# Clustered attention and an MLP on one core: the weighted values of a pair of heads in one run

## The chip, the core and the metric

The kernel runs on one core of a Trainium2 chip. Its time is the device time of one execution in microseconds (us). Three runs of the kernel before took 932.9, 934.0 and 934.55 us, median 934.0. One more execution was profiled.

The engines have these names in the profile: PE is TensorE (PEld its weight loads), DVE VectorE, ACT ScalarE, POOL GpSimd, SP SyncE, which here only starts transfers.

## The reference

Four batches, eight heads, 768 positions, 64 elements a head. Queries and keys are each assigned to the nearest of 16 centroids of their head; a query sees only the keys of its own cluster. The result, 512 wide, goes through a mix over the positions of rank 32 and an MLP of 512 to 2048 to 512.

```python
mask = q_assign[:, :, :, None] == k_assign[:, :, None, :]
scores = np.where(mask, scale * (q @ k.T), -1e9)
attn = exp(scores - max(scores)); attn = attn / (sum(attn) + 1e-9)
x = attn @ v                                  # all heads side by side: (4, 768, 512)
u = x + (xt @ U @ V).T                        # xt is x transposed, the mix over positions
out = u + np.maximum(u @ w_ch1, 0.0) @ w_ch2
```

## The kernel before

Two heads of one batch make a pair; 16 pairs (0 to 15) are worked through one after the other, four to a batch. For one pair the steps are these, each a small function of the kernel:

- `load` fetches the queries and keys into the tile R, `load_v` the values into vt. `split_hi` and `split_lo` split R into a rounded part and its remainder (in the tile arena, L797 and L802), and the `place_` functions move rows of it by transfers on SyncE's queue.
- `sims` (L760) multiplies by the centroids, and `clusters` (eight steps on VectorE, L770 to L789) makes one-hot rows of the nearest one. These rows are added to keys and queries, so that a pair of one cluster scores far above all others.
- `rowmax` (L875) computes scores of 128 queries by 384 keys for the maximum of each query, which VectorE takes from the bank (L877), 24 times a pair. `rowmax_T` and `rowmax_place` turn the maxima (L887) into a row of the operands of `scores`.
- `scores` (L899, L901) computes 128 keys by 768 queries in four matmuls, and ScalarE takes the exp into a buffer pr (L904), 12 times a pair.
- `values` (L922) multiplies an exp by the values: two matmuls side by side in the array, 64 columns each, into the bank o_ps. Six of them, one for each 128 keys, add up to half a pair. `weights` (L914, GpSimd mostly) adds up the exps for the denominators in the tile T.
- `sums`, `sums_T` (L934, L942) and `normalise` (L955, L956) finish the pair; `turn_x` and `store_x` write it out. For each batch, `mix_u`, `mix_sum` and `mix_v` follow (L980 to L1005).

Row maxima and scores read operands of the type fp32r and use the whole array. Values, similarities and sums are f32, and 64 or 32 columns wide; several run side by side. Transposes are f32 with the whole array. The profile lists an f32 matmul that is not a transpose as two records.

What is left of the banks of the accumulator by the scores (two buffers of two banks) are four banks, in turn for row maxima, values, similarities, sums and transposes (`work`).

Behind the attention stands the MLP of batch 0 (`gemm1`, `after_gemm1`, `gemm2`), then the other three batches with weights that are combined in between (`seven1`, `seven2` and their helpers).

The order of everything is written out by hand. Each step is an event with a time in steps of the plan; 12 steps are one pair, M0 (193) is where the MLP begins. The tables `times`, `mixes` and `stages` give a base time by step and kind of pair, and `shifts` moves single events. The events are sorted by time and issued in that order, and each engine keeps it: an engine waits at the head of its queue, and all behind it wait as well. In this plan the values of a pair stand in two groups, one behind each six scores, and the row maxima of the next pair are spread between the scores by the list `spots`.

Of the kernel before, what the change touches and what calls it, by code (L numbers as in the profile page):

```python
# [59 lines left out]
    "load0":           (-34.78, -31.87, -43.62,   None,   None, -25.08),  # L60
    "load1":           (-26.35, -29.08, -32.88,   None,   None, -24.23),
    "sims":            ( -25.34, -28.59, -28.55,   None,   None, -21.62),
    "place_clusters":  (-17.02, -15.36, -15.03, None, -8.7, -12.43),
    "split_hi0":       (-29.17, -30.78, -24.16,   None,   None, -23.84),
    "split_lo0":       (-23.33, -24.18, -23.58,   None,   None, -18.16),
    "split_hi1":       (-23.81, -24.01, -24.25,   None,   None, -18.05),
# [5 lines left out]
    "load_v":          ( -19.68,  -4.35,  -7.21,   None, -23.16,  -9.16),  # L72
    "rowmax":          (-14.93, -14.94, -14.87, -5.2, -8.0, -11.36),
    "rowmax_T":        (-3.27, -3.31, -3.81, 0.8, 0.23, -2.00),
    "rowmax_place":    (-2.26, -2.12, -2.82, 1.0, 1.84, -1.34),
    "scores":          (     0,  -0.95,  -0.37,  -1.30,   0.99,   0.07),
    "weights":         (  1.45,  -0.11,   0.32,   0.76,   3.19,   1.68),
    "values":          (  1.45,   1.51,   0.02,   1.05,   3.14,   2.27),
    "sums":            ( 14.31,  14.69,  13.43,  15.42,  15.27,  14.98),
    "sums_T":          ( 15.73,  15.65,   14.20,  16.05,  17.52,  16.44),  # L80
    "normalise0":      ( 21.14,  17.04,  14.88,  21.88,  20.90,  21.40),
    "normalise1":      ( 22.35,  16.83,  15.64,   27.11,  21.03,  19.88),
    "clusters":        (-23.85, -25.21,  -23.10,   None,   None, -20.35),
# [13 lines left out]
    "g0":   ( 34.93,  36.55,  42.58,  52.94),  # L97
# [10 lines left out]
    "scores 14 1 3": -0.9,  # L108
    "turn_x 7 1": 0.26,
    "recover 7 1 1 0": 0.52,  # L110
    "mix_T 1 3 1": 0.27,
    "clusters 2 4": -0.66,
    "turn_u 0 3": 1.01,
    "values 5 1 0": -1.54,
    "rowmax 6 3 1": -4.17,
    "rowmax 10 2 0": -1.29,
    "normalise 6 1": -3.47,
    "clusters 3 7": 2.95,
    "scores 11 1 4": 0.73,
# [12 lines left out]
    "scores 2 0 0": 0.47,
    "split_lo 4 0": 0.77,
    "seven2 3 3 6": -0.13,
    "rowmax 2 4 0": -0.71,
    "rowmax_place 15 0 12": -0.73,
    "fetch_w2 6 0 3 4 5": -0.15,
    "load_mix 0 3": 1.15,
    "load_weights 1 6 3": 0.37,
    "scores 9 0 0": 0.29,  # L140
    "normalise 14 0": -1.4,
    "recover 7 1 1 1": 0.22,
    "load_weights 1 0 2": 1.44,
    "scores 14 1 4": -0.69,
    "rowmax 3 8 0": 0.26,
    "turn_x 7 0": 0.24,
    "fetch_w2 7 0 3 4 5": 0.19,
    "rowmax 3 5 1": 2.44,
    "rowmax 3 3 1": -0.83,
    "normalise 12 0": -0.59,  # L150
    "scores 15 1 2": -0.7,
    "values 5 0 0": -0.29,
    "values 5 0 1": -0.29,
    "values 5 0 2": -0.29,
    "values 5 0 3": -0.29,
    "values 5 0 4": -0.29,
    "values 5 1 1": -0.29,
    "values 5 1 2": -0.29,
    "values 5 1 3": -0.29,
    "values 5 1 4": -0.29,  # L160
    "rowmax 2 1 0": -0.55,
    "rowmax 3 3 0": -0.22,
    "rowmax 5 7 0": 2.33,
    "clusters 11 0": -1.58,
    "scores 12 1 1": 0.42,
    "scores 3 0 4": -0.07,
    "rowmax 3 1 1": 0.87,
    "sums 14": 0.54,
    "scores 10 1 1": -0.12,
    "clusters 15 1": -0.21,  # L170
    "rowmax 13 1 0": -1.15,
    "split_lo 7 0": 0.66,
    "normalise 4 0": -1.22,
    "load_weights 1 2 3": -0.16,
    "rowmax 6 8 0": 1.78,
# [1475 lines left out]
```

## Time and profile before

| | |
|---|---|
| median of three runs | 934.0 us (932.9 to 934.55) |
| profiled execution | 933.45 us |
| its span, first to last instruction | 931.6 us |
| TensorE busy | 910.3 us, 98% |
| VectorE busy | 733.7 us, 79% |
| GpSimd busy | 607.7 us, 65% |
| ScalarE busy | 449.2 us, 48% |
| mean granted clock of TensorE | 0.988 |
| moved by transfers | 206.26 MB |

Busy time is the time in which an engine has an instruction under way. A matmul's record overlaps the next one, so the time that one takes up in the queue is read from the start of one row to the start of the next. All durations come from the one profiled execution, so a sum is made against its 933.45 us.

### The profile page before, as it was taken

The numbers are of one execution on the slowest core, as the hardware profiler recorded it, in microseconds if no ns is written. First come the engines' busy times: TensorE is split into PE (matmuls) and PEld (weight loads), VectorE is DVE, ScalarE is ACT, GpSimd is POOL, SyncE is SP. The second block draws the span as 40 slices with busy tenths as digits, with TensorE's granted clock in tenths as the row PEclk, the third lists the DMA queues.
The fourth block names the chain that finished last, engine by engine and source line by source line (L and its number), as shares of the span: only waits on it lengthen the run. The fifth ranks groups of instructions, "written<-read, shape, count | busy, mean of one in ns | idle before, by whom it ended". The sixth has DMA issues, their size and how long they took to land.

```text
span 931.6 us, 15094 instructions
## 1 busy us (share of the span) xinstructions
PE 910.3 (98%) x5157; PEld 756.2 (81%) x5157; DVE 733.7 (79%) x1391; ACT 449.2 (48%) x803; POOL 607.7 (65%) x459
## 2 busy tenths in 40 slices
PE   5899999999999999999999999999999999999997
PEld 1666666776666666767899999999999999999997
DVE  6899888888888887698866355767879778887777
ACT  6454554555555545566656533542435424263330
POOL 3467687889789987773457936832487524865333
PEclk7899999999999999999999999999999999999999
DMA  7485655676768674368989997798776998679643
GB/s 210 109 203 129 185 132 123 206 186 172 198 156 190 175 185 112 92 204 275 281 283 318 291 324 266 263 338 269 236 281 211 355 252 311 231 254 327 234 174 114
DMA packets 122925, 206.26 MB, mean 221 GB/s; under 512 B 46528, under 2 KB 90240, under 8 KB 118368
## 3 DMA queue, kind: packets, MB, share of 16 engines
q1 hardware_dynamic: 122464, 205.20, 71.8%
q8 instruction: 41, 0.67, 0.3%
q14 instruction: 36, 0.29, 0.1%
q10 hardware_dynamic: 384, 0.10, 0.0%
HBM read 131.96 MB, written 42.83 MB: 188 GB/s over the span
## 4 chain that ended last, share of the span: by engine, by line
PE 93%; DVE 4%; DMA 2%; ACT 1%; issue 1%; SPq 0%; DVEq 0%; ACTq 0%
PE o_ps L922 14%; PE ps_max L875 8%; PE st L899 7%; PE st L901 6%; PE ps_p L1289 3%; PE ps_p L1290 3%; PE ps_p L1291 3%; PE ps_q L1365 3%; PE ps_q L1366 3%; PE ps_q L1367 3%; PE ps_q L1289 3%; PE ps_q L1291 3%; PE ps_q L1290 3%; PE ps_p L1365 3%; PE ps_p L1367 3%; PE ps_p L1366 3%
## 5 line engine op out<-in xcount | busy, mean ns | idle before, releaser
L914 POOL TENSOR_TENSOR T<-T,pr 128x768 f32<-128x768 f32 x120 | 223.9, 1866 | 31.5 <-ACT pr L904 11.3
L877 DVE TENSOR_REDUCE m<-ps_max 128x1 f32<-128x384 f32 x384 | 195.0, 546 | 45.3 <-PE ps_max L875 43.4
L904 ACT ACTIVATE pr<-st 128x768 f32<-128x768 f32 x192 | 154.6, 812 | 90.7 <-PE st L901 76.9
L922 PE MATMUL o_ps<-pr,vt 128*64 128x384 f32 x768 | 133.6, 492 | 0.1
L875 PE MATMUL ps_max<-arena 128*128 128x384 f32 x384 | 121.1, 380 | 8.5 <-DVE arena L840 6.2
L875 PEld LDWEIGHTS ps_max<-arena 128*128 128x128 f32 x384 | 70.5, 196 | 51.5 <-DVE m L877 18.1
L899 PE MATMUL st<-arena 128*128 128x384 f32 x384 | 103.3, 350 | 0.4 <-ACT pr L904 0.3
L922 PEld LDWEIGHTS o_ps<-pr,vt 128*64 128x64 f32 x768 | 51.2, 136 | 64.6 <-issue 60.3
L901 PE MATMUL st<-arena 97*128 97x384 f32 x384 | 98.9, 339 | 0.6 <-DMA arena<-mT 0.6
L914 POOL TENSOR_TENSOR T<-pr 128x768 f32<-128x768 f32 x30 | 56.1, 1869 | 47.3 <-ACT pr L904 47.3
L899 PEld LDWEIGHTS st<-arena 128*128 128x128 f32 x384 | 66.9, 189 | 7.8 <-issue 2.4
L901 PEld LDWEIGHTS st<-arena 97*128 97x128 f32 x384 | 70.6, 189 | 0.9 <-DMA arena<-mT 0.9
L1289 PE MATMUL ps_p<-arena,w 128*128 128x384 f32 x186 | 62.2, 334 | 0.0
L1291 PE MATMUL ps_p<-arena,w 128*128 128x384 f32 x186 | 62.2, 334 | 0.0
L1290 PE MATMUL ps_p<-arena,w 128*128 128x384 f32 x186 | 62.2, 334 | 0.0
L926 ACT COPY os<-o_ps 128x384 f32<-128x384 f32 x32 | 15.4, 481 | 78.1 <-PE o_ps L922 78.0
L1289 PE MATMUL ps_q<-arena,w 128*128 128x384 f32 x150 | 50.2, 335 | 0.0
L1291 PE MATMUL ps_q<-arena,w 128*128 128x384 f32 x150 | 50.2, 334 | 0.0
L1290 PE MATMUL ps_q<-arena,w 128*128 128x384 f32 x150 | 50.1, 334 | 0.0
L802 POOL TENSOR_TENSOR arena<-R,arena 128x768 fp32r<-128x768 f32 x16 | 35.0, 2186 | 15.7 <-ACT arena L797 15.6
L1351 POOL TENSOR_TENSOR h<-ring,h 128x384 fp32r<-128x384 f32 x17 | 17.7, 1041 | 38.6 <-ACT h L1341 19.6
L1290 PEld LDWEIGHTS ps_p<-arena,w 128*128 128x128 f32 x186 | 34.9, 188 | 0.1
(580 smaller groups left out, 2363.0 us busy)
## 6 DMA issues: line engine op xcount, KB each, us to landing
w<-wc SPq DMA_DIRECT2D x24, 1024.0 KB
w<-wc SPq DMA_DIRECT2D x25, 768.0 KB
arena<-wc SPq DMA_DIRECT2D x19, 768.0 KB
rw<-in_w SPq DMA_DIRECT2D x27, 512.0 KB
R<-in_qk SPq DMA_DIRECT2D x32, 384.0 KB
arena<-arena SPq DMA_DIRECT2D x31, 384.0 KB
arena<-arena SPq DMA_DIRECT2D x62, 192.0 KB
wc<-f SPq DMA_DIRECT2D x46, 256.0 KB
```

Of the source, the lines that this page charges most:

```text
L875: nc.tensor.matmul(ps[:, 0:HS], x1[:, 0, g // 2, g % 2, t * P:(t + 1) * P], x1[:, 1, h, g % 2, :], start=True, stop=True)
L877: nc.vector.reduce_max(live["m2", i][:, h, u:u + 1], ps[:, 0:HS], axis=AX.X)
L899: nc.tensor.matmul(st[:, j, 0:HS], x1[:, 1, hk, j, ks], x1[:, 0, h, j, :], start=True, stop=False)
L901: nc.tensor.matmul(st[:, j, 0:HS], x2[0:97, 1, hk, j, ks], x2[0:97, 0, h, j, :], start=False, stop=True)
L904: nc.scalar.activation(pr, st[:, :, 0:HS], AF.Exp, scale=SCALE)
L914: eng.tensor_add(T, live["p", i, h, 0] if c == 1 else T, live["p", i, h, c])
L922: nc.tensor.matmul(o_ps[64 * j:64 * j + 64, 0:HS], vv[:, c, j, :], pr[:, j, :], start=(c == 0), stop=(c == NT - 1))
L1289: nc.tensor.matmul(ps, w[:, 0, k], u[:, 0, k], start=(k == 0), stop=False)
L1290: nc.tensor.matmul(ps, w[:, 0, k], u[:, 1, k], start=False, stop=False)
L1291: nc.tensor.matmul(ps, w[:, 1, k], u[:, 0, k], start=False, stop=(k == 1))
L1365: nc.tensor.matmul(ps, w[:, 0], h[:, 0], start=(j == 0), stop=False)
L1366: nc.tensor.matmul(ps, w[:, 0], h[:, 1], start=False, stop=False)
```

## The change

The exps of a pair get twelve buffers in place of eleven, and the values two in place of three. From pair 3 to pair 13 the values of a pair stand together at step 11.5 of the pair, behind its twelve scores. The row maxima of pairs 4 to 14 come at an even pace of 0.41 steps from the start of the pair before, the eight cluster steps of a pair directly one behind the other. The base times change for the first pairs and for others, and the table `shifts` grows from about 420 entries to some 1570, up to the middle of batch 0's MLP. No instruction is added or removed, and none changes its engine.

```diff
-    "sims":            ( -25.34, -28.59, -28.55,   None,   None, -21.62),
+    "sims": (-24.51, -24.51, -24.51, None, None, -21.62),
...
-    "normalise0":      ( 21.14,  17.04,  14.88,  21.88,  20.90,  21.40),
+    "normalise0": (23.2, 17.04, 14.88, 21.88, 20.90, 23.2),
...
-    "scores 14 1 3": -0.9,
+    "scores 14 1 3": -2.38745455,
...
-        live["v", i] = sb.tile([P, NT, 2, D], F32, name="vt", bufs=3)
+        live["v", i] = sb.tile([P, NT, 2, D], F32, name="vt", bufs=2)
...
-        pr = sb.tile([P, 2, HS], F32, name="pr", bufs=11)
+        pr = sb.tile([P, 2, HS], F32, name="pr", bufs=12)
...
+    RUN, ROW0, PACE, LO, HI = 11.5, 0.33, 0.41, 3, 13
...
-                at(when("clusters", i) + 0.7 * k, clusters, i, k)
+                at(when("clusters", i) + (0.7 if i < 3 else 0.02) * k, clusters, i, k)
...
+                elif LO < i <= HI + 1:
+                    at(NS * (i - 1) + ROW0 + PACE * (2 * u + h), rowmax, i, u, h)
...
-            at(when("values", i) + GV * (k // GV) + GV - 1 + 0.03 * (k % GV), values, i, h, c)
+            if LO <= i <= HI:
+                at(NS * i + RUN + 0.005 * k, values, i, h, c)
+            else:
+                at(when("values", i) + GV * (k // GV) + GV - 1 + 0.03 * (k % GV), values, i, h, c)
```

TensorE's order around the values of pair 7, first of the kernel before. L899 and L901 are scores, L875 a row maximum, L760 the similarity of a later pair, L922 the values.

```order
L875 MATMUL ps_max<-arena 128x384 x2
L760 MATMUL ps_sim<-R,cT 32x384 x4
L875 MATMUL ps_max<-arena 128x384
L899 MATMUL st<-arena 128x384 x2
L901 MATMUL st<-arena 128x384 x2
L875 MATMUL ps_max<-arena 128x384 x2
L899 MATMUL st<-arena 128x384 x2
L901 MATMUL st<-arena 128x384 x2
L875 MATMUL ps_max<-arena 128x384
L922 MATMUL o_ps<-pr,vt 64x384 x12
L875 MATMUL ps_max<-arena 128x384 x2
```

The same place in the changed kernel; L2052 and L2054 are scores there, L2028 a row maximum, L2040 the transpose of the maxima, L1913 the similarity, L2075 the values.

```order
L2052 MATMUL st<-arena 128x384 x2
L2054 MATMUL st<-arena 128x384 x2
L2028 MATMUL ps_max<-arena 128x384 x2
L2040 MATMUL ps_mT<-ident,m 12x128
L1913 MATMUL ps_sim<-R,cT 32x384 x4
L2075 MATMUL o_ps<-pr,vt 64x384 x24
L2028 MATMUL ps_max<-arena 128x384 x2
L2052 MATMUL st<-arena 128x384 x2
```

Twelve matmuls of half a pair, with the similarity apart, have become 24 of a whole pair with the similarity and the transpose right before them.

VectorE's order for the clusters of pair 10, first before: L770 to L786 are cluster steps, L802 a split, L877 a row maximum.

```order
L770 STREAM_TRANSPOSE ps_sim<-ps_sim 128x384
L802 TENSOR_TENSOR arena<-R,arena 128x768
L776 TENSOR_REDUCE most<-ps_sim 128x24
L877 TENSOR_REDUCE m_2600<-ps_max 128x1 x2
L780 TENSOR_TENSOR ps_sim<-ps_sim,most 128x384
L877 TENSOR_REDUCE m_2600<-ps_max 128x1
L782 TENSOR_TENSOR ps_sim<-ps_sim,rank 128x384
L877 TENSOR_REDUCE m_2600<-ps_max 128x1 x2
L776 TENSOR_REDUCE most<-ps_sim 128x24
```

And in the changed kernel, beside the run of pair 7; L1745 to L1748 unpack a piece of weights, L1955 is the split, L2030 a row maximum.

```order
L1923 STREAM_TRANSPOSE ps_sim<-ps_sim 128x384
L1929 TENSOR_REDUCE most<-ps_sim 128x24
L1933 TENSOR_TENSOR ps_sim<-ps_sim,most 128x384
L1935 TENSOR_TENSOR ps_sim<-ps_sim,rank 128x384
L1929 TENSOR_REDUCE most<-ps_sim 128x24
L1939 TENSOR_TENSOR oh<-ps_sim,most 128x12x16 x2
L2120 STREAM_TRANSPOSE xs_2624<-xt 128x384
L1745 TENSOR_SCALAR ps_t<-rw_g 128x512
L1746 SCALAR_TENSOR_TENSOR ps_t<-rw_g,ps_t 128x512
L1748 SCALAR_TENSOR_TENSOR rw_t<-rw,ps_t 128x512
L1955 TENSOR_TENSOR arena<-R,arena 128x768
L2030 TENSOR_REDUCE m_2532<-ps_max 128x1 x2
```

The reductions that stood between the cluster steps have moved away; weights and split stand behind the steps instead.

At the start of the program TensorE's order was this (L694 turns the centroids, L887 the maxima of pair 0).

```order
L694 MATMUL ps_c<-ident,rw_g 128x128
L760 MATMUL ps_sim<-R,cT 32x384 x4
L875 MATMUL ps_max<-arena 128x384 x4
L694 MATMUL ps_c<-ident,rw_g 128x128
L875 MATMUL ps_max<-arena 128x384 x4
L694 MATMUL ps_c<-ident,rw_g 128x128
L875 MATMUL ps_max<-arena 128x384 x2
L760 MATMUL ps_sim<-R,cT 32x384 x4
L694 MATMUL ps_c<-ident,rw_g 128x128
L875 MATMUL ps_max<-arena 128x384 x2
```

In the changed kernel L1847 turns the centroids, L1913 is the similarity, and L2052 the first score.

```order
L1847 MATMUL ps_c<-ident,rw_g 128x128
L1913 MATMUL ps_sim<-R,cT 32x384 x4
L1847 MATMUL ps_c<-ident,rw_g 128x128
L1913 MATMUL ps_sim<-R,cT 32x384 x4
L1847 MATMUL ps_c<-ident,rw_g 128x128
L2028 MATMUL ps_max<-arena 128x384 x12
L1847 MATMUL ps_c<-ident,rw_g 128x128
L2028 MATMUL ps_max<-arena 128x384
L2040 MATMUL ps_mT<-ident,m 6x128
L2028 MATMUL ps_max<-arena 128x384 x2
L1847 MATMUL ps_c<-ident,rw_g 128x128
L2028 MATMUL ps_max<-arena 128x384 x3
```

The second similarity has moved ahead of the row maxima of pair 0, and twelve of these stand together. Up to the first scores nine more row maxima follow in the kernel before, and none beyond these rows in the changed one.

## Rows read from the trace of the kernel before

**Rows 1.** The page's busy times: us (share of the span) and instructions of each engine.
```profile
PE 910.3 (98%) x5157; PEld 756.2 (81%) x5157; DVE 733.7 (79%) x1391; ACT 449.2 (48%) x803; POOL 607.7 (65%) x459
```
**Rows 2.** Stages: us, busy PE, PEld, DVE, ACT, POOL (instructions), clock, DMA share, GB/s.
```profile
200.00:250.00 50.00, 50.00 (x310) 34.48 (x311) 44.68 (x90) 28.39 (x42) 44.70 (x25) 1.00 0.70 191
500.00:550.00 50.00, 50.00 (x254) 45.52 (x253) 22.01 (x38) 22.78 (x43) 39.35 (x31) 1.00 1.00 293
```
**Rows 3.** The values' line: count, ns min/median/max, first and last start.
```profile
L922 PE MATMUL o_ps<-pr,vt x768: 486/486/537, 38.8 to 430.2; 128*64 128x384 f32 x192
```
**Rows 4.** TensorE's timeline around half a pair's values: start us, us, engine, line, tiles, records.
```profile
331.27 0.55 PE L955 MATMUL ps_oT<-ident,os 128*128 128x128 f32 x3
331.58 0.59 PE L899 MATMUL st<-arena 128*128 128x384 f32 x2
332.01 0.52 PE L901 MATMUL st<-arena 97*128 97x384 f32 x2
332.37 0.52 PE L875 MATMUL ps_max<-arena 128*128 128x384 f32 x2
332.82 4.09 PE L922 MATMUL o_ps<-pr,vt 128*64 128x384 f32 x24
336.84 0.62 PE L875 MATMUL ps_max<-arena 128*128 128x384 f32 x2
337.30 0.51 PE L899 MATMUL st<-arena 128*128 128x384 f32 x2
```
**Rows 5.** The same timeline at a short run of values.
```profile
68.22 0.87 PE L922 MATMUL o_ps<-pr,vt 128*64 128x384 f32 x4
69.02 0.44 PE L875 MATMUL ps_max<-arena 128*128 128x384 f32 x1
```
**Rows 6.** The same timeline at transposes between fp32r matmuls.
```profile
202.86 0.49 PE L955 MATMUL ps_oT<-ident,os 128*128 128x128 f32 x3
203.10 0.42 PE L875 MATMUL ps_max<-arena 128*128 128x384 f32 x1
203.36 0.27 PE L887 MATMUL ps_mT<-ident,m 128*12 128x128 f32 x1
```
**Rows 7.** The same timeline at transposes in front of values.
```profile
127.77 0.49 PE L955 MATMUL ps_oT<-ident,os 128*128 128x128 f32 x3
128.23 0.87 PE L922 MATMUL o_ps<-pr,vt 128*64 128x384 f32 x4
```
**Rows 8.** Two windows of the first 70 us, columns as in rows 2.
```profile
14.00:24.00 10.00, 8.43 (x26) 4.07 (x26) 7.09 (x15) 5.93 (x17) 5.77 (x16) 0.50 0.94 259
60.00:70.00 10.00, 9.79 (x57) 7.50 (x56) 9.90 (x25) 6.24 (x10) 8.36 (x5) 1.00 0.72 199
```
**Rows 9.** VectorE's waits from 14 to 65 us: us in total, times, longest.
```profile
DVE m L877 <- PE ps_max L875: 3.8, 8, 1.6
DVE ps_sim L770 <- PE ps_sim L760: 1.2, 1, 1.2
```
**Rows 10.** The page's groups, GpSimd's adds: busy us, mean ns, idle before.
```profile
L914 POOL TENSOR_TENSOR T<-T,pr 128x768 f32<-128x768 f32 x120 | 223.9, 1866 | 31.5 <-ACT pr L904 11.3
```
**Rows 11.** VectorE's groups by line, 100 to 400 us: busy us, mean ns, idle before.
```profile
L877 DVE TENSOR_REDUCE m<-ps_max 128x1 f32<-128x384 f32 x286 | 146.2, 546 | 38.0 <-PE ps_max L875 36.3
L802 DVE TENSOR_TENSOR arena<-R,arena 128x768 fp32r<-128x768 f32 x11 | 16.7, 1518 | 0.0
...
L789 DVE STREAM_TRANSPOSE ohT<-oh 128x768 f32<-128x768 f32 x11 | 10.6, 965 | 0.0
...
L593 DVE SCALAR_TENSOR_TENSOR ps_t<-rw_g,ps_t 128x512 int32<-128x512 int32 x10 | 7.0, 696 | 0.3
```
**Rows 12.** VectorE on the similarity's bank: window, us, busy (instructions), clock, DMA share, GB/s.
```profile
200.00:250.00 50.00, 6.78 (x14) 1.00 0.70 191
```
**Rows 13.** TensorE's longest waits from 65 to 440 us: us in total, times, longest.
```profile
PE st L901 <- DMA arena<-mT: 0.6, 1, 0.6
```
**Rows 14.** TensorE's timeline at the first scores.
```profile
29.88 0.84 PE L899 MATMUL st<-arena 128*128 128x384 f32 x2
```

More of the change, by code (lines that the diff above doesn't have):

```diff
@@ L145 @@
[L145 to L146 removed]
+    "load_weights 1 0 2": 0.6475,
+    "scores 14 1 4": -1.111875,
+    "rowmax 3 8 0": -2.24,
     "fetch_w2 7 0 3 4 5": 0.19,
[L148 to L175, printed above, removed]
-    "clusters 3 6": -0.52,
-    "sums_T 14": 0.99,
@@ new lines @@
+    "rowmax 3 11 0": -0.39361111,
+    "rowmax 3 4 1": 3.48,
+    "weights 2 1 1": 0.238,
+    "scores 2 1 4": -2.8975,
+    "rowmax 3 7 1": -4.95005556,
+    "scores 2 0 5": 2.11175926,
+    "rowmax 3 7 0": 2.67263889,
+    "values 2 0 0": -0.07550926,
+    "split_hi 5 0": 1.75666667,
+    "load_v 4": 19.38333333,
+    "sums_T 1": 2.1184375,
+    "rowmax 3 9 1": 1.13078704,
+    "rowmax 4 1 1": 4.85333333,
+    "rowmax 4 3 0": 1.46466667,
+    "load 6 0": -9.8356,
+    "load_mix 2 3": 2.67080128,
@@ new lines @@
+    "rowmax 10 8 1": -6.225,
+    "rowmax 10 0 0": 0.78318182,
+    "scores 9 0 2": -0.88818182,
+    "rowmax 10 9 1": -4.01166667,
+    "rowmax 10 5 1": -3.72,
+    "rowmax 10 7 1": 2.17909091,
+    "rowmax 10 10 0": -0.00922078,
+    "store_x 7 1": 9.04083333,
+    "rowmax 10 2 1": 6.34824675,
+    "rowmax 10 4 0": 4.565,
+    "rowmax 10 0 1": 0.35,
+    "load 13 0": -4.20974026,
+    "scores 9 1 0": 4.44666667,
+    "weights 8 1 5": 0.65636364,
+    "sums 8": -0.78333333,
+    "rowmax 10 7 0": -5.47905303,
@@ new lines @@
+    "values 9 0 3": 0.30045455,
+    "values 9 0 4": 0.30863636,
+    "values 9 0 5": 0.31681818,
+    "normalise 8 1": 0.65113636,
+    "rowmax 11 4 1": 5.36636364,
+    "rowmax 11 2 1": -2.3305,
+    "place_keys_lo 12": -5.03852273,
+    "place_queries 12": -4.30113636,
+    "scores 10 0 1": -1.07909091,
+    "weights 9 1 2": 2.85375,
+    "weights 9 1 3": 1.9415,
+    "rowmax 11 11 0": -9.32213333,
+    "load 14 0": -2.16076923,
+    "rowmax 11 2 0": -2.05897727,
+    "rowmax 11 9 0": -7.494,
@@ new lines @@
+    "values 1 1 5": -0.02,
+    "scores 2 1 1": -4.4212,
+    "scores 2 1 0": 1.12171296,
+    "weights 2 0 3": 2.50986111,
+    "weights 2 0 4": 7.419375,
+    "values 2 0 1": -0.0946875,
+    "values 2 0 2": -0.123125,
+    "normalise 1 1": -0.495,
+    "load 6 1": 6.07111111,
+    "values 2 1 0": -0.1903125,
+    "values 2 1 1": -0.1809375,
+    "values 2 1 2": -0.19125,
+    "values 2 1 3": -0.07730769,
+    "weights 2 1 2": -0.686,
+    "values 2 1 4": -0.1000641,
+    "values 2 1 5": -0.12644231,
@@ new lines @@
+    "scores 5 0 2": -1.03571429,
+    "rowmax 6 9 1": -1.22533333,
+    "values 5 1 0": -0.63,
+    "scores 6 0 0": 2.37125,
+    "rowmax 8 5 0": -11.96305455,
+    "rowmax_T 7 0 12": -5.59991169,
+    "scores 7 0 3": -3.0834375,
+    "weights 7 0 1": -2.205,
+    "sums 6": -2.53,
+    "scores 7 1 2": 3.34625,
+    "clusters 10 5": 0.00872727,
+    "rowmax 9 3 1": -2.79090909,
+    "scores 8 0 2": -0.658125,
+    "weights 8 0 2": -2.069375,
+    "scores 8 0 3": -1.17142857,
+    "weights 8 0 4": -2.77857143,
```

1851 lines of the change are left out of this document (1477 added, 374 removed).

## The prediction

> **What bounds the kernel now.** I read the page's busy shares first: TensorE is busy 910.3 of 931.6 us [rows 1]. A share of the whole span says little about a stage, so the table of stages came next. From the middle of the attention part to its end TensorE works through whole windows (50.00 of 50 us at 200 to 250), at a granted clock of 1.00, while VectorE has 44.68 and GpSimd 44.70 us in the same window [rows 2]. In the MLP stage at 500 to 550 it is again 50.00 of 50, with the DMA engines at a share of 1.00 [rows 2]. So the end of the program is set by the length of TensorE's own queue nearly everywhere, and an order can only win what is lost between its matmuls. Two places lose something: the seams between kinds of matmul (below), and the first 70 us, where TensorE is not the limit. Sixteen pairs of heads pass in 38.8 to 430.2 us [rows 3], 24.5 us each; VectorE and GpSimd fill some 0.89 of that, so neither is far behind.
>
> **What a seam costs.** In the timeline of TensorE two fp32r matmuls of 384 columns take 0.36 us from start to start (332.01 to 332.37). The same two in front of the values take 0.45 (332.37 to 332.82), and directly behind the values 0.46 (336.84 to 337.30) [rows 4]: 0.09 us on the way in, 0.10 behind the way out. A run of values has a fixed part as well. 24 records last 4.02 us [rows 4], 4 records 0.80 [rows 5], so a record costs (4.02 - 0.80) / 20 = 0.161 us and every run 0.80 - 4 x 0.161 = 0.16 us on top. One stretch of values between fp32r matmuls thus loses 0.35 us. Similarities and sums, 32 columns wide, I take to behave alike.
>
> The Trainium skill, TensorEngine Tiling (Array Packing), Key Properties, says that a change of the tiling mode drains the engine. The trace agrees: the losses sit at both ends of a run, and by that rule and by the rows alike a run twice as long pays once.
>
> Transposes between fp32r matmuls cost 0.24 for three and 0.08 on the next matmul (0.26, against half of 0.36), 0.32 in all [rows 6]. Directly behind tiled matmuls three cost 0.31 and 0.07 (331.27 to 332.01 [rows 4], with 0.36 taken off the last two), so 0.06 more. In front of values they cost 0.46 (127.77 to 128.23 [rows 7]), 0.14 more. Moving a transpose to the edge of a run is therefore not free, and that enters the sum.
>
> **The change part by part.**
> *Runs.* I counted seams in the two orders of TensorE over the whole program. Steps from fp32r into tiled matmuls fall from 66 to 39, steps from tiled into fp32r from 68 to 35, runs of tiled matmuls of one kind from 84 to 68. In exchange steps from a transpose into tiled matmuls rise from 7 to 14, and from tiled into a transpose from 5 to 18. By the rows: 27 x 0.09 = 2.4, 33 x 0.10 = 3.3 and 16 x 0.16 = 2.5 us are saved, 7 x 0.14 = 1.0 and 13 x 0.06 = 0.8 are paid. Sum: 6.4 us less in TensorE's queue. Since these windows hold no idle time, all of it should move the end, if nothing else is late.
>
> *Startup.* From 14 to 24 us VectorE is busy 7.09 of 10 us [rows 8], and its reductions waited 3.8 us for TensorE's row maxima and 1.2 us for a similarity between 14 and 65 us [rows 9]. In the first order the transposes of the centroids and the second similarity stand among the row maxima; in the new one twelve row maxima follow one another, and 18 instead of 21 stand ahead of the first scores. From 60 to 70 us VectorE is busy 9.90 of 10 [rows 8], so until then it is the bound and what it gains is kept. At most those 5.0 us can go; against that, ScalarE now has more copies ahead of the one-hot rows, and the second pair's rows are loaded behind the first V, which could cost as much as the 1.5 us of one split. I take 2.0, two thirds of the idle 2.9 us of the window at 14 to 24, with ends at -1.5 and 5.0.
>
> *Twelve buffers of exps, two of V.* With a run per pair all twelve exps of a pair live until the run, and the first exp of the next pair needs the first buffer back just after the run has begun. GpSimd's sums read them too: ten adds of 1.87 us [rows 10], 18.7 of the pair's 24.5 us, and the first exp of the next pair needs only the first of them, which is done before the run. The third buffer of V goes: a load now waits for the run two pairs earlier, and stands behind it in the new order, some 20 us ahead of its use. Both cost nothing as long as the load's wait doesn't hold SyncE's queue; behind it stand the moves of key and query rows for the next pairs, and the row maxima wait for those.
>
> *VectorE in the run.* What changes most is when VectorE works. Reductions of 0.546 us [rows 11] now come in blocks with the scores, and the eight cluster steps, the split and the unpacking of weights stand in one block beside the run. For pair 7 (the first is 0) the block is 3.4 us on the similarity's bank (6.78 for two pairs [rows 12]), 0.97 for the transpose, 1.52 for the split and 3 x 0.70 for the unpacking [rows 11]: 8.0 us. TensorE's run covers 48 x 0.161 + 0.16 = 7.9 us and a similarity 0.8. That fits closely. Between two runs 24 reductions need 13.1 us, and TensorE has 72 matmuls of 0.18 us, a sum and some transposes, about 15 us. The waits of TensorE in the old order are small here (the longest group, 0.6 us in all [rows 13]); I add 1.0 us for the closer fit. Its bounds are 0 and the 11 us of the third rival.
>
> *The MLP's first half.* Its matmuls are regrouped, but TensorE has no idle time there [rows 2] and the records are the same; nothing.
>
> **Sum.** On the profiled execution: 933.45 - 6.4 - 2.0 + 1.0 = 926.05. The median of the runs shown stands 0.55 higher, so 926.6 us.
>
> **Rivals.**
> *More than that: about 922.* VectorE's startup waits go in full (5.0 instead of 2.0) and no new waits come: 934.0 - 6.4 - 5.0 = 922.6. For it speaks that twelve reductions follow each other; against it that ScalarE's copies and the moves by DMA end that stage too.
>
> *The time comes back as waits: about 932.* VectorE and GpSimd fill 0.89 of a pair [rows 2], and without the seams 0.92. If one of them sets the pace in the scores' part, TensorE saves 6.4 us in its queue and waits as long; the startup's 2.0 stays: 932. Against it: there are 2 us a pair still free on each. The Trainium skill, TensorEngine Tiling (Array Packing), PSUM Bottleneck, warns that tiling quickens TensorE but not the engines that empty its banks; this is the form that it would take here, and the trace so far shows VectorE keeping up.
>
> *Slower: about 938.* After a run TensorE can issue only as many row maxima as banks are free (four, shared with values, sums and similarities). If VectorE comes to the run with four reductions left (2.2 us) and then does its 8.0 us, it is back after 10.2 us; similarity, run, a transpose and the next two row maxima cover 0.8 + 7.9 + 0.1 + 0.4 = 9.2. A wait of 1.0 us in each of eleven runs is 11 us: 934.0 - 6.4 - 2.0 + 1.0 + 11 = 937.6. It decides from 0.7 us a run on, where the 7.4 us are used up. For it: the sum is that near. Against it: the cluster's bank comes free before the block's end.
>
> *The change doesn't do what it says.* Three of the eleven runs are still cut in two by a transpose; that is in the counts, so it moves neither the sum nor a chance.
>
> **How the numbers follow.** Forecast (923 to 930): 0.52. More: 0.14. Waits: 0.17, a third of it still over 0.2% faster and the rest within. Slower: 0.17. A measurement of this kernel tells no change from about 0.2%, 1.9 us. Faster 0.52 + 0.14 + 0.06 = 0.72, within 0.11, slower 0.17. The range from 919 to 937 takes in the startup's bounds and most of the slower case; about 0.14 is left out, mostly above. The likeliest case alone spans 923 to 930.
>
> **What would show it.** In the profile after, the values of one pair stand in one row of 48 records of about 7.9 us; the seams' row maxima keep their 0.45 and 0.46; the first scores start before 29.88 us [rows 14]; the window at 200 to 250 still shows 50 us of TensorE. A wait of a row maximum for VectorE right after each run would show the third rival, a busy TensorE with fewer us in its queue but the same end the second. I am wrong if the in-run cost of 0.16 is not per run, or if the first scores start no earlier.

## The result, and the profile after

The changed kernel takes 920.8 us (median of four runs, 919.86 to 921.67), against 934.3 for the kernel before on the same chip (932.9 to 935.09): ratio 0.9857, 95% interval 0.984 to 0.9874. It is 13.5 us faster. The forecast was 926.6, so the sign was right and the likeliest size was little more than half; the time lies in the range, near its lower end.

The profiled execution took 920.11 us, its span 918.3. The page's busy times, us with share and instructions:

```profile
PE 897.4 (98%) x5157; PEld 761.4 (83%) x5157; DVE 738.0 (80%) x1391; ACT 452.8 (49%) x803; POOL 602.7 (66%) x459
```

The instructions are the same in number as in [rows 1], and TensorE is at 98% in both. The 12.9 us that left its busy time are therefore not work: the records of two neighbours run into each other, so what is lost between two matmuls counts as busy too. One whole pair shows it. TensorE's timeline, columns as in [rows 4]; L1913 is a similarity, L2075 the values, L2028 a row maximum, L2052 a score:

```profile
218.65 0.51 PE L1913 MATMUL ps_sim<-R,cT 128*32 128x384 f32 x4
219.08 7.96 PE L2075 MATMUL o_ps<-pr,vt 128*64 128x384 f32 x48
226.97 0.62 PE L2028 MATMUL ps_max<-arena 128*128 128x384 f32 x2
227.43 0.51 PE L2052 MATMUL st<-arena 128*128 128x384 f32 x2
```

48 records stand in one row and take 219.08 to 226.97, 7.89 us in the queue; twice the half run of [rows 4] is 8.04. The two row maxima behind it take 0.46 as they did there: a seam costs what it cost, there are fewer of them.

To see where the time came from I marked the same event in both traces (us from the span's start):

| | before | after | gained so far |
|---|---|---|---|
| first score | 29.88 | 27.52 | 2.36 |
| last value of pair 0 | 56.93 | 53.37 | 3.56 |
| last value of pair 1 | 86.49 | 82.55 | 3.94 |
| last value of pair 15 | 430.23 | 415.19 | 15.04 |
| first matmul of the MLP | 430.64 | 415.60 | 15.04 |
| last matmul of its first half | 567.06 | 553.62 | 13.44 |
| last matmul of all | 926.05 | 912.10 | 13.95 |

So the start gives 3.9 us, the pairs 2 to 15 give 11.1, and the MLP's first half takes 1.6 back.

The stages, columns as in [rows 2] and [rows 8]; four lines of after:

```profile
14.00:24.00 10.00, 8.61 (x25) 4.29 (x17) 8.37 (x19) 7.51 (x15) 4.42 (x16) 0.50 0.62 160
30.00:40.00 10.00, 9.86 (x57) 6.19 (x57) 9.90 (x22) 4.94 (x7) 6.92 (x4) 1.00 0.73 190
200.00:250.00 50.00, 49.17 (x312) 34.89 (x310) 46.13 (x88) 28.60 (x42) 43.65 (x24) 1.00 0.65 175
500.00:550.00 50.00, 48.45 (x244) 43.62 (x243) 25.77 (x41) 23.80 (x46) 32.85 (x26) 1.00 1.03 321
```

From 14 to 24 us VectorE is busy 8.37 us where it was 7.09, and from 30 to 40 it is full (9.90). Where [rows 2] had two windows without idle time on TensorE, both now miss something: 0.83 us at 200 to 250, and 1.55 us at 500 to 550. These are two single waits. TensorE's timeline at the first; the bracket is the idle time and what ended it:

```profile
203.13 0.34 PE L2028 MATMUL ps_max<-arena 128*128 128x384 f32 x1
204.30 0.41 PE L2028 MATMUL ps_max<-arena 128*128 128x384 f32 x1 [0.83 <-ACT pr L2057]
```

and VectorE's at the same place:

```profile
193.65 0.55 DVE L2030 TENSOR_REDUCE m<-ps_max 128x1 f32<-128x384 f32 x1
194.43 0.60 DVE L1923 STREAM_TRANSPOSE ps_sim<-ps_sim 128x384 f32<-128x384 f32 x1 [0.23 <-PE ps_sim L1913]
...
199.46 2.56 DVE L1955 TENSOR_TENSOR arena<-R,arena 128x768 fp32r<-128x768 f32 x1
201.95 0.68 DVE L1745 TENSOR_SCALAR ps_t<-rw_g 128x512 int32<-128x512 int32 x1
202.67 0.70 DVE L1746 SCALAR_TENSOR_TENSOR ps_t<-rw_g,ps_t 128x512 int32<-128x512 int32 x1
203.47 0.69 DVE L1748 SCALAR_TENSOR_TENSOR rw_t<-rw,ps_t 128x512 int32<-128x512 int32 x1
204.07 1.24 DVE L2030 TENSOR_REDUCE m<-ps_max 128x1 f32<-128x384 f32 x2
```

The second row maximum behind the run of pair 6 goes off 0.14 us after VectorE has ended its block (203.47 + 0.69 = 204.16). The profile names ScalarE; two runs below lose this wait, one in which VectorE has less to do and one in which the join of weights (the three steps from 201.95 on) stands elsewhere, so it is for VectorE's block. TensorE waits for a block that is too long, in one run of eleven and at the third rival's price of 1.0 us, but not in the way that the rival gave: VectorE had no reductions left over, for its last one ended at 194.20, before the run began at 194.43. The block itself takes 9.7 us (194.43 to 204.16) where the prediction had 8.0, with the split at 2.56 us in place of the mean of 1.52 [rows 11]. The second wait, at 504 us:

```profile
504.25 0.34 PE L2210 MATMUL ps_h<-u,arena 128*128 128x384 f32 x1
506.14 0.50 PE L2227 MATMUL y<-w,hx 128*128 128x512 f32 x1 [1.54 <-ACT hx L2216]
```

Here the second gemm waits for ScalarE's relu. On ScalarE the relu stands behind splits that wait for transfers, and once for GpSimd:

```profile
500.41 0.62 ACT L2297 CAST f<-f 128x512 fp32r<-128x512 f32 x1 [3.18 <-DMA wc<-f]
502.34 0.62 ACT L2297 CAST rw_t<-f 128x512 fp32r<-128x512 f32 x1 [0.82 <-DMA wc<-rw_t]
505.07 0.62 ACT L2297 CAST rw_t<-f 128x512 fp32r<-128x512 f32 x1 [2.11 <-POOL f L2301]
505.60 0.48 ACT L2216 ACTIVATE hx<-ps_h 128x384 fp32r<-128x384 f32 x1
```

VectorE's waits from 14 to 65 us, the answer to [rows 9]: 5.0 us have become 2.6, not nothing.

```profile
DVE m L2030 <- PE ps_max L2028: 2.4, 3, 1.3
DVE ps_sim L1923 <- PE ps_sim L1913: 0.2, 1, 0.2
```

**The pairs 2 to 15, taken apart.** I sorted every step from one record's start to the next by the kinds of the two (C tiled, T transpose, R fp32r), from the last value of pair 1 to that of pair 15:

| step | before: count, mean ns | after: count, mean ns |
|---|---|---|
| R to C | 53, 282 | 28, 268 |
| C to R | 55, 416 | 26, 412 |
| first R to R behind C | 54, 281 | 25, 285 |
| C to T | 3, 417 | 14, 409 |
| T to C | 5, 209 | 12, 203 |
| R to T | 53, 200 | 27, 190 |
| T to R | 51, 39 | 29, 28 |
| T to T | 98, 112 | 110, 115 |
| first R to R behind T | 46, 259 | 28, 261 |
| first C to C behind R or T | 58, 7 | 40, 7 |
| other C to C | 804, 141 | 840, 141 |
| other R to R | 767, 182 | 865, 178 |

All steps together go from 343.74 to 332.63 us. The changed counts at the old means make -7.85 us of that, the changed means -3.26, of which the other R to R have 2.8 (865 x 3.2 ns). Those 2.8 are single waits: above the usual 174 ns, steps of 230 ns and more add up to 4.2 us in before (30 of them) and 1.4 in after (7, the one at 203 us the largest). So three terms are to be tested: seams, start, and small waits that went.

The small waits of before show on TensorE's weight loads, three of them here (the time in the bracket is that of the load unit):

```profile
259.50 0.19 PEld L901 LDWEIGHTS st<-arena 97*128 97x128 f32 x1 [0.89 <-DMA arena<-mT]
412.48 0.30 PEld L899 LDWEIGHTS st<-arena 128*128 128x128 f32 x2 [0.58 <-ACT pr L904]
314.66 0.19 PEld L875 LDWEIGHTS ps_max<-arena 128*128 128x128 f32 x1 [0.21 <-DVE m L877]
```

Summed by the name in the bracket, 2.1 of the 4.2 us are put down to VectorE (1.7 to its row maxima), 1.0 to ScalarE and 0.8 to the transfer that brings the row of maxima; 0.2 have none.

### The profile page after: what moved, and what is told of

Read it like the earlier page. It is cut to its first block, busy times and chain, and to the rows that moved or that the text cites. A ratio compares the mean times of both kernels' runs of the same rounds, so it can differ in the third digit from the quotient of the medians.

```text
span 918.3 us, 15004 instructions
## 1 busy us (share of the span) xinstructions
PE 897.4 (98%) x5157; PEld 761.4 (83%) x5157; DVE 738.0 (80%) x1391; ACT 452.8 (49%) x803; POOL 602.7 (66%) x459
## 4 chain that ended last, share of the span: by engine, by line
PE 95%; ACT 2%; DMA 2%; DVE 1%; SPq 0%; issue 0%; ACTq 0%; DVEq 0%
PE o_ps L2075 14%; PE ps_max L2028 8%; PE st L2052 7%; PE st L2054 7%; PE ps_q L2520 4%; PE ps_q L2518 4%; PE ps_q L2519 4%; PE ps_p L2443 4%; PE ps_p L2442 4%; PE ps_p L2444 4%; PE ps_p L2520 3%; PE ps_p L2518 3%; PE ps_p L2519 3%; PE ps_q L2442 3%; PE ps_q L2444 3%; PE ps_q L2443 3%
## 5 line engine op out<-in xcount | busy, mean ns | idle before, releaser
L2030 DVE TENSOR_REDUCE m<-ps_max 128x1 f32<-128x384 f32 x384 | 191.8, 548 | 19.0 <-PE ps_max L2028 15.9
L2075 PE MATMUL o_ps<-pr,vt 128*64 128x384 f32 x768 | 130.0, 490 | 0.0
L2028 PE MATMUL ps_max<-arena 128*128 128x384 f32 x384 | 110.4, 364 | 1.9 <-ACT pr L2057 0.8
L2075 PEld LDWEIGHTS o_ps<-pr,vt 128*64 128x64 f32 x768 | 52.7, 137 | 68.3 <-issue 61.7
L2052 PE MATMUL st<-arena 128*128 128x384 f32 x384 | 102.2, 347 | 0.0
L2054 PE MATMUL st<-arena 97*128 97x384 f32 x384 | 98.7, 338 | 0.0
L2028 PEld LDWEIGHTS ps_max<-arena 128*128 128x128 f32 x384 | 71.4, 195 | 20.9 <-DVE m L2030 9.8
L2052 PEld LDWEIGHTS st<-arena 128*128 128x128 f32 x384 | 68.4, 189 | 4.4 <-issue 2.4
L2054 PEld LDWEIGHTS st<-arena 97*128 97x128 f32 x384 | 71.0, 189 | 0.0
L1955 POOL TENSOR_TENSOR arena<-R,arena 128x768 fp32r<-128x768 f32 x16 | 30.4, 1899 | 29.3 <-ACT arena L1950 29.2
```

The source lines that it names most:

```text
L2028: nc.tensor.matmul(ps[:, 0:HS], x1[:, 0, g // 2, g % 2, t * P:(t + 1) * P], x1[:, 1, h, g % 2, :], start=True, stop=True)
L2030: nc.vector.reduce_max(live["m2", i][:, h, u:u + 1], ps[:, 0:HS], axis=AX.X)
L2052: nc.tensor.matmul(st[:, j, 0:HS], x1[:, 1, hk, j, ks], x1[:, 0, h, j, :], start=True, stop=False)
L2054: nc.tensor.matmul(st[:, j, 0:HS], x2[0:97, 1, hk, j, ks], x2[0:97, 0, h, j, :], start=False, stop=True)
L2075: nc.tensor.matmul(o_ps[64 * j:64 * j + 64, 0:HS], vv[:, c, j, :], pr[:, j, :], start=(c == 0), stop=(c == NT - 1))
```

## The experiments

Each kernel's time stands beside runs of the kernel before on the same chip (medians 934.0 to 934.8). Changes of order are given by the events. From one execution to the next the start and the MLP differ by 1 to 2 us, but in the pairs 2 to 15 three more executions with the changed kernel's order there take 332.58, 332.59 and 332.61 us, so differences of some 0.3 us count in that stretch.

**The start alone, from both sides.** First the changed kernel with its first 183 events in the old order:

> The changed kernel, with its first 183 events (all up to the last values of pair 0) put back into the order that the kernel before has for them. Theory: the start alone gave 3.6 us (the last value of pair 0 ended at 53.4 in place of 56.9 us), because VectorE no longer waited among the centroid transposes, and nothing later makes up for it: 920.8 + 3.6 = 924.4 us, and pair 0's last value again near 57 us. Rival: VectorE is the bound until 70 us in either order, so the later pairs catch up: 921 to 922 us.

Measured: 926.3 us (926.16 to 927.14), ratio 0.9918, 0.9904 to 0.9932. Then the old order (and its buffers, eleven and three) with the new start:

> The kernel before (its order, its eleven buffers of exps and three of V), with the 183 events of the start in the order of the changed kernel. Theory: the start is worth its 3.6 us here as well: 934.3 - 3.6 = 930.7 us. Rival: the old order behind it is not ready earlier (its reductions and transfers are placed for the old start): 933 to 934 us.

Measured: 932.6 us (931.21 to 933.96), ratio 0.9983, 0.9974 to 0.9992.

| us | old start, new rest | new start, old rest |
|---|---|---|
| first score | 33.07 | 27.21 |
| last value of pair 0 | 59.51 | 52.86 |
| last value of pair 1 | 89.28 | 83.79 |
| pair 1 to pair 15 | 332.58 | 345.08 |

With the new rest the pairs take 332.6 us whatever went before (332.64 in the changed kernel): nothing catches up, the rival of the first run is out. But the first run overstates the start, for its first score comes 3.2 us later than in the kernel before. ScalarE's order there is not that of before; a load of its table, which stands at 23.58 us in before, came early:

```profile
15.74 1.28 ACT L1838 ACT_TABLE_LOAD   x1
```

It stands ahead of the turning of the centroids, which TensorE's row maxima then wait behind. The start's worth is therefore read from before against after: 3.9 us. In nine executions below and above with the new start and the new rest, the last value of pair 1 stands at 81.9 to 83.1 us. The second run gains 4.1 at pair 0, keeps 2.7 at pair 1 and 1.4 at the end: under the old order more than half of it is lost again, 1.3 us of that in the pairs 2 to 15. To which waits is open.

**Runs cut by scores.** The changed kernel, in eight whole runs one score of the next pair moved into the middle:

```diff
 values 7 0 1
+scores 8 0 0
 values 7 0 2
...
 rowmax 9 2 0
-scores 8 0 0
```

> The changed kernel, with the first scores of the next pair (four fp32r matmuls) moved into the middle of the values, in the eight pairs whose run is whole. Nothing else moves. Theory of the seams: each cut costs 0.09 in front, 0.16 in the run and 0.10 behind, 0.35 us: 8 x 0.35 = 2.8, 923.6 us. Rival: the seams were hidden and the gain comes from fewer waits alone: 920.8, within 0.5.

Measured: 926.8 us (926.27 to 928.3), ratio 0.9926, 0.9913 to 0.9938. And three in each:

> As cut1, with three scores of the next pair put into each of the eight runs (behind the 5th, 7th and 10th of its twelve values). Theory of the seams: three times as much, 24 x 0.35 = 8.4, 929.2 us. Rival that the seams are hidden: 921 to 922 us. A third possibility, that an early score waits for its row of maxima, would show as a wait of st for a DMA at the first cut.

Measured: 945.2 us (943.12 to 946.27), ratio 1.0117, 1.0102 to 1.0133. Both cost more than the seams. By the table of steps the seams have 3.1 and 9.1 us (0.38 to 0.39 each), and waits 3.1 and 14.2. TensorE's timeline with three:

```profile
235.84 1.09 PE L2028 MATMUL ps_max<-arena 128*128 128x384 f32 x4
...
239.71 1.30 PE L2028 MATMUL ps_max<-arena 128*128 128x384 f32 x3
```

and its waits from 70 to 440 us:

```profile
PE st L2054 <- DMA arena<-mT: 3.5, 4, 1.1
```

Behind the run the row maxima have lost the scores that stood between them, so three or four follow one another and wait for VectorE (the weight loads of row maxima that wait for its reductions go from 6.2 to 13.9 us in total between 70 and 440 us); and scores that come earlier wait for the row of maxima that a transfer brings. Neither belongs to a seam, so these two runs did not settle its price.

**Runs cut by nothing.** The same places, but only a matmul of zeros put in, and no instruction moved:

```diff
+        if (i, h, c) in CUTS:
+            nc.tensor.matmul(o_ps[:, 0:32], zero, zero[:, 0:32], start=False, stop=False)
```

> The changed kernel with one more matmul in the middle of the run of weighted values of eight pairs (8 in all): a full-array fp32r matmul of a 128x128 tile of zeros by 32 columns of zeros, added into the open accumulation. It adds nothing to the values; one GpSimd memset of the zeros is added at the start; no other instruction moves. Each cuts a run in two and so adds one entry to the tiled mode, one exit and one run's fixed part and no transposed or moved scores. Theory (a cut costs the seam itself, 0.35 us by the rows of before, plus some 0.02 to 0.05 us for the 32 columns): 8 x 0.38 = +3.0, 920.8 -> 923.8 (bounds 923.2 to 924.5). Rival 1 (in the run that moved one score into each of eight runs and lost 6.0 us, only waits made the price; a seam is hidden under the weight loads): under +1.0, below 921.8. Rival 2 (a longer run gives VectorE time that its block beside the run needs, so half of a seam comes back as a shorter wait behind the run): +1.5, 922.3.

> The same with three such matmuls of zeros in each of the eight runs, at the places where three scores stood in the earlier run (24 in all, one of them moved aside where a value's row ended). Theory: 24 x 0.38 = +9.1, 920.8 -> 929.9 (bounds 928.5 to 931.2), the dose linear: three times what eight cost. Rival 1 (seams hidden): under +3, below 923.8. Rival 2 (VectorE gets its time back): 8 runs x at most 1.0 us of it, so +5 to +6, 926. The three scores cost 24.4 us; what this run leaves of that (some 15 us) is the part of the waits, for VectorE's row maxima and for the query's transposes, and not of the change of mode.

Measured: 925.0 us (923.16 to 925.78), ratio 0.9898, 0.9883 to 0.9913, with eight cuts; 927.2 us (927.0 to 927.67), ratio 0.9926, 0.9913 to 0.994, with 24. The same run as above, with one cut and with three:

```profile
218.97 4.09 PE L2080 MATMUL o_ps<-pr,vt 128*64 128x384 f32 x24
222.99 0.28 PE L2083 MATMUL o_ps<-zero 128*128 128x32 f32 x1
223.21 4.09 PE L2080 MATMUL o_ps<-pr,vt 128*64 128x384 f32 x24
227.23 0.62 PE L2033 MATMUL ps_max<-arena 128*128 128x384 f32 x2
```

```profile
219.56 2.16 PE L2080 MATMUL o_ps<-pr,vt 128*64 128x384 f32 x12
221.65 0.28 PE L2083 MATMUL o_ps<-zero 128*128 128x32 f32 x1
...
226.46 2.16 PE L2080 MATMUL o_ps<-pr,vt 128*64 128x384 f32 x12
228.55 0.62 PE L2033 MATMUL ps_max<-arena 128*128 128x384 f32 x2
```

The run takes 8.26 us with one cut (218.97 to 227.23) and 8.99 with three, against 7.89 without: 0.37 a cut. Summed over all cuts the steps give 0.364 in both doses (2.91 for eight, 8.74 for 24). That is the 0.35 of the prediction's rows and a little for the 32 columns. A cut is not quite a seam, though. Its way out is that of a seam (0.416 us from the last value's start to the zeros, and 0.416 to a row maximum at the end of the run), and so is the slower first step behind it (0.367 in place of 0.316). But the 0.214 from the zeros to the next value stand in for a seam's way in and for the slow first row maximum behind it, and they hold the weight load of the zeros as well. A matmul of zeros that changes no mode was not run, so what the change of mode alone takes of the 0.214 is not separated.

The whole time is less clean. Pairs 2 to 15 grow by 2.6 and 7.7 us, three times as much for three times the cuts; VectorE's wait at 203 us gives back 0.3 of 2.9 and 1.0 of 8.7 (rival 2 had about half). The rest is a start 0.4 to 0.6 us earlier, and in the run with eight the wait at the MLP, 2.3 us instead of 1.5. Eight cuts measured above the theory's bounds, 24 below. The profiled execution with eight took 923.16, the fastest of its four; what made the other three longer no trace shows.

**VectorE with less to do.** Two of eight cluster steps left out, in both kernels:

```diff
+        if i > 1 and k in (3, 4):
+            return
```

> The kernel before, without two of VectorE's steps of the clusters of pairs 2 to 15: the multiplication by the ranks and the second maximum, which break ties (0.57 + 0.56 = 1.13 us of VectorE a pair, 15.8 us in all); which cluster an equal maximum goes to is then not computed as in the reference. No other instruction moves. Theory (TensorE's small waits in the pairs are for VectorE, which is late behind the runs; the change made them fewer by setting more scores between the row maxima): VectorE is 1.1 us less late, TensorE gets back part of it in every pair: 934.3 -> 930.8 (bounds 927.5 to 932.8). Rival (those gaps are the weight loads' own pace, and VectorE's lateness is covered): 933.8 to 934.8.

> The same two steps left out of the changed kernel. Theory (the change has already taken most of these waits away, the weight loads that wait for a row maximum going from 10.4 to 6.2 us): 920.8 -> 919.0 (bounds 917.5 to 920.2), so that the two kernels stand some 11.5 to 12 us apart instead of 13.5; that the distance shrinks by over 1 is what tells that some of the gain came through VectorE. Rival 1 (VectorE covered in both): 920.3 to 921.3 and the distance stays. Rival 2 (VectorE holds the changed kernel more, its block beside a run being one piece): gains more than the kernel before does, below 917.

Measured: 934.1 us (932.72 to 935.26), ratio 1.0002, 0.9993 to 1.0011; and 920.3 us (919.42 to 920.4), ratio 0.9854, 0.9841 to 0.9868. The one-hot rows are then no longer those of the reference; the instructions behind them are the same. The theory falls, the first rival holds: pairs 2 to 15 become 0.6 us shorter in the kernel before (the steps of 230 ns and more go from 4.2 to 3.5 us, 0.4 of it at the transfer) and 1.1 in the changed one, which is just the wait at 203 us. There the split took 1.86 us instead of 2.56, so the block was 1.8 us shorter and not 1.13. The old order's small waits were not VectorE's arrears from the clusters. That the changed kernel's whole time falls by 0.5 and not by 1.1 is the MLP's doing: in this execution it takes 498.30 us where the changed kernel's profile has 496.50, its wait is 1.77 us, and from 506.7 to 510.1 us the granted clock is 0.50, the lower level of 1.2 GHz.

**The two waits.** The two stores that stand between those that ScalarE waits for, put back:

```diff
+store_block 1 2 A11 0
 load_weights 3 3 3
...
+store_block 1 2 A12 0
 split_low 2 2
...
 store_sum 3 1 3 0
-store_block 1 2 A12 0
 store_sum 3 1 3 1
...
-store_block 1 2 A11 0
 store_block 1 3 A22 0
```

> The changed kernel with two events put back to where the kernel before has them: the stores of two blocks of batch 1 (A11 and A12) that stand on SyncE's queue ahead of the stores that ScalarE's split waits for in the first half of the MLP. Nothing else moves. Theory (TensorE's wait of 1.5 us at 504 us, second gemm on ScalarE's relu, comes from that queue alone): the wait goes, 920.8 -> 919.2 (918.8 to 919.6). Rival (the blocks' stores now stand where they delay something else, or the gemms are fed by DMA there): 920.5 to 921.0, and the trace shows another wait of over 1 us between 500 and 560 us.

Measured: 919.2 us (919.11 to 919.87), ratio 0.984, 0.9827 to 0.9854. The wait is gone:

```profile
504.54 0.34 PE L2210 MATMUL ps_h<-u,arena 128*128 128x384 f32 x1
504.75 0.50 PE L2227 MATMUL y<-w,hx 128*128 128x512 f32 x1
```

From the MLP's first matmul to the last of all it is 494.83 us, against 496.50 in the changed kernel and 495.41 in the one before. This stretch doesn't repeat well: with the two stores moved it takes 496.4 to 498.6 us in seven executions and the wait 1.2 to 2.3; with them back 494.8 here and 496.0 in the run below with the join moved on, where 0.54 us of the wait remain. And with all of the MLP in the old order:

> The changed kernel with all events behind the last weighted value of pair 15 in the order of the kernel before (the change's order up to there, so the attention part is the changed one). Theory (the new order of the MLP's first half holds no gain, and one loss, the 1.5 us wait): as the run above, 919.2 (918.8 to 919.8). Rival (the new order there does bring part of the 13.5 us): slower than the changed kernel, 921.5 or more.

Measured: 918.5 us (917.9 to 919.24), ratio 0.9832, 0.9818 to 0.9845. The MLP part takes 495.41 us, and 495.4 to 495.6 in three executions of the kernel before and its variants. That the two stores cost time is shown by the wait that went and by the median, 1.6 lower (1.7 in this stretch of the two profiles). That the rest of the new order gains 0.6 there (495.41 to 494.83) is not shown, since the run with the join moved on has 496.0. In the profiled executions this kernel ends 0.7 below the one with the stores alone because of its start (first score at 27.05, there 27.72), which differs between executions of one order by some tenths of a us. Both are faster than the changed kernel.

**The join moved on.** The same, and the join at 201.95 us moved out of VectorE's block to between row maxima:

```diff
-load_weights 0 3 2
 values 6 0 5
...
 rowmax 8 6 1
+load_weights 0 3 2
```

> The changed kernel with the stores of the two blocks put back (919.2) and one join of a weight part (three VectorE instructions, 2.05 us) moved out of VectorE's block beside the run of pair 6 to behind six more row maxima. Theory (the wait of about 1.0 us at 203 us, the second row maximum behind that run, comes from the block's length alone, and between the row maxima, which come at half of VectorE's pace, the join is covered): 918.3 (917.7 to 918.9), and the distance from the last value of pair 6 to that of pair 7 goes from 24.66 to 23.7. Rival (the row maxima in between then wait as long as the one did): 919.2, the distance within 0.2 of 24.66.

Measured: 920.1 us (919.39 to 920.77), ratio 0.9854, 0.984 to 0.9867. The theory falls, and the rival's mechanism goes further than its size: from pair 6's last value to pair 7's it is 25.3 us, neither 23.7 nor the rival's 24.66. The wait at 203 us went, another came at once:

```profile
208.31 0.52 PE L2028 MATMUL ps_max<-arena 128*128 128x384 f32 x2
...
209.37 0.52 PE L2028 MATMUL ps_max<-arena 128*128 128x384 f32 x2
...
211.42 0.45 PE L2028 MATMUL ps_max<-arena 128*128 128x384 f32 x1 [0.82 <-DVE rw_t L1748]
```

The step of the expectation that was wrong: row maxima come two at a time, every 1.06 us (208.31 to 209.37), and that is nearly VectorE's pace, as its timeline in the changed kernel shows there:

```profile
205.62 2.55 DVE L2030 TENSOR_REDUCE m<-ps_max 128x1 f32<-128x384 f32 x5 [0.31 <-PE ps_max L2028]
```

Five reductions in 2.55 us are 1.02 for two. Between row maxima there is next to no cover.

**The join without a bank.** That wait names the join's last step, which gives back one of the four banks. So, with the stores put back, the join in its own tile in SBUF:

```diff
-        b = (pool["y"].tile(...) if in_bank else work("ps_t")).bitcast(I32)[0:r, 0:n]
+            b = t = raw.tile([P, 512], I32, name="rw_t")[0:r, 0:n]
```

> The changed kernel with the stores of the two blocks put back (919.2), and the join of a weight part in the attention part working in its own tile in SBUF; in the changed kernel its first two steps write to one of the four banks that row maxima, values, similarities and sums take in turn. No instruction is added, removed or moved. Theory (the third rival's mechanism is one of banks: in the run before, a row maximum waited 0.82 us and the profile named the join's last step, which gives its bank back; the wait of 0.83 us at 203 us has a join in front of it too): the wait at 203 us shrinks to under 0.4 and the distance from the last value of pair 6 to that of pair 7 goes from 24.66 to 24.1 or less; 918.6 (918.0 to 919.1). Rival 1 (the wait is for VectorE's next reduction, whatever the banks): 24.66 as before and 919.2. Rival 2 (three steps of the join in SBUF take longer beside GpSimd's adds than 0.68 us each, by up to the 2.56 against 0.96 us that a split shows): slower, 919.8 to 922.

Measured: 960.9 us (960.06 to 963.02), ratio 1.0289, 1.0275 to 1.0303. Rival 2, far beyond its size. VectorE at the end of the run of pair 6:

```profile
216.16 2.04 DVE L1747 TENSOR_SCALAR rw_t<-rw_g 128x512 int32<-128x512 int32 x1
218.23 2.21 DVE L1748 SCALAR_TENSOR_TENSOR rw_t<-rw_g,rw_t 128x512 int32<-128x512 int32 x1
220.47 2.20 DVE L1750 SCALAR_TENSOR_TENSOR rw_t<-rw,rw_t 128x512 int32<-128x512 int32 x1
```

and TensorE's waits from 70 to 460 us:

```profile
PE ps_max L2030 <- DVE m L2032: 10.1, 7, 3.1
PE ps_sum L2089 <- DVE m L2032: 2.9, 1, 2.9
```

From 70 to 450 us the three steps take 78.2 us in place of 35.2, 43.0 more, and pairs 2 to 15 take 34.7 more (367.3). Not all of that is VectorE's directly. Six times in the pairs, for 20.5 us in all, TensorE's granted clock is at 0.50, the lower level; just before each it had waited 1.6 to 3.1 us. Two other waits, of 1.8 and 2.0 us, were not followed by it. One of the six stretches:

```profile
195.90:199.30 3.40, 3.40 (x11) 3.12 (x11) 1.72 (x5) 1.18 (x2) 0.77 (x1) 0.50 0.90 273
```

Two scores there take 0.64 us from start to start, 0.35 elsewhere; half of 20.5 us, some 10, is about the most that these stretches can have cost (an estimate from those rows). What the bank alone is worth stays open, since the price of the steps covers it. But the run shows the other side of the lighter kernels: some 13.6 us (12 x 1.13) taken off VectorE bring 1.1, and 43.0 put on it cost 34.7, by that estimate some 24 or more of them without the clock.

## Why the prediction was right, and where not

*Bound.* Right: the end moved by what left TensorE's queue, and the 50.00 us windows [rows 2] were the reason to trust it. The sign that I named for it, 50 us again at 200 to 250, did not come: 49.17, by the one wait at 203 us.

*Seams, 6.4 us.* Right in kind, a little small. The changed counts of steps are worth 7.85 us in pairs 2 to 15 by the table; where the 1.5 more sit was not taken apart. The means of a seam hardly moved (282 to 268, 416 to 412 ns), their number halved, so the loss is paid per change, and a cut put in costs 0.364 us where the rows gave 0.35, with the reserve made above. The Trainium skill, TensorEngine Tiling (Array Packing), Key Properties, says that a change of the tiling mode drains the engine; the trace agrees in that the loss goes with the number of changes.

*Startup, 2.0 us.* Mis-sized: 3.9 by the last value of pair 1. I took two thirds of VectorE's idle time at 14 to 24 us. Its waits fell by 2.4 of 5.0 and the first score came 2.36 us earlier, near my value; the other 1.6 us came behind it, 1.2 of them by the last value of pair 0, while VectorE is now full from 30 on (9.90 of 10). The mean granted clock at 30 to 40 us is 1.00 there, the level of 2.4 GHz throughout, and was 0.91:

```profile
30.00:40.00 10.00, 9.80 (x55) 7.58 (x53) 8.44 (x18) 5.54 (x8) 5.97 (x4) 0.91 0.40 101
```

Both kernels are at the lower level of 1.2 GHz (0.50) at 14 to 24 us, with TensorE busy 8.43 [rows 8] and 8.61 of 10 us; the changed one leaves it before 30 us, the other after. I had not looked at that, but it is not what made the difference. The kernel with the join moved on has the changed kernel's order up to there, and in its execution the lower level lasts beyond 30 us as well:

```profile
30.00:40.00 10.00, 10.00 (x56) 7.36 (x57) 9.68 (x21) 4.94 (x7) 6.18 (x4) 0.90 0.72 190
```

Its first score stands at 27.44 us and its last value of pair 1 at 83.13, 0.6 later than in the changed kernel. So by these two executions the clock has at most some 0.6 of the 3.9 us.

*New waits, +1.0 us.* This step failed, in sign. TensorE's small waits became fewer by 2.8 us, the one new wait at 203 us included. I had taken the old waits for small from a view that shows the longest group as 0.6 us [rows 13]; but a short wait of a weight load need not show as idle time of the matmuls (at 314.66 the load waits 0.21 us and the matmul shows none), and 30 steps that were each 0.06 to 0.73 us too long made 4.2 us. By the profile half of them wait for VectorE, the rest for ScalarE and a transfer. They are not its arrears, since leaving out 1.13 us of VectorE a pair took only 0.6 of it; that they went because the new order sets more scores between the row maxima is likely and was not tested by itself.

*The third rival.* A block longer than its cover does make TensorE wait, and of eleven runs one met it. What made it longer was not four reductions left over but the split, which I had put at its mean of 1.52 us: in before, the splits between 100 and 400 us take from 0.93 to 2.35, and the one at 199.46 took 2.56. The lighter kernel shows the margin: that wait went, no other was there to go. The runs with scores moved and the dear join show how thin the cover is that I had worked out (8.0 us against 7.9 and 0.8).

*Buffers.* I said nothing is lost by them. No wait for a load of V shows in the trace; apart from the order they were not tried.

*The MLP, nothing.* Wrong by 1.1 us in this execution, lost through two stores on SyncE's queue; a gain by the rest is not shown. I read that TensorE was full there and did not look at what the moved stores stand in front of.

Together: -7.85 - 3.26 - 3.94 + 1.60 - 0.51 = -13.96 at the last matmul, where the forecast had -7.4. Of the 6.6 us between, 4.3 lie between the +1.0 of new waits and the -3.26 of the changed means, 1.9 are the start and 1.5 the seams; the MLP takes 1.1 back. That the time still lies in the range owes something to the range's width, which was set for the start and for the third rival and not for waits that go.

## What to carry to other kernels

Where one engine fills whole windows, count the changes of mode in its queue and price one from the steps between starts: a number taken so at three rows held against a dose of 8 and of 24, as far as a cut stands for a seam. Price a block by its longest step and not by a mean, where another engine can slow the step. Small waits must be summed from the steps between starts too, since weight loads hide them from the views of idle time. Of an order that is moved, follow the stores and the engine that stands nearest to its own limit: on VectorE 13.6 us less brought 1.1, and 43.0 more cost 34.7, with a lower clock of TensorE behind some of its waits.

## What was not expected of the hardware

The join's steps, which take 0.70 us (L1746, median 0.695) with one operand in the accumulator's bank, take 2.19 us in the median with all operands in SBUF, beside GpSimd's adds; the fastest of them takes 0.69. The step with a single input, from SBUF to SBUF (L1747, 128x512), takes from 0.38 to 2.04 us, where it takes 0.65 to 0.70 into a bank: faster at best and three times as long at worst. The split of two SBUF operands, 0.96 us at the start, where GpSimd did nothing, is 2.56 us at 199.46. The Trainium skill, SBUF — State Buffer, Who interferes with whom, says that a VectorE instruction with two SBUF inputs contends with a GpSimd instruction that reads SBUF, that one in a mode that takes two ports contends with GpSimd as well, and that the later one blocks until the first has ended. The trace agrees in kind; adds of 1.8 to 2.1 us beside steps of 2.0 to 2.2 are what one step waiting for one add would look like.
